# A state-space layer with a feed-forward behind it: opening loads reordered, the first state's sums in banks of their own, and block 1's first products moved

## Chip, cores and metric

One NeuronCore of a Trainium2 chip. The time is device time in microseconds of one execution of the whole program; the figure given for a kernel is the median of its runs. Engines are named as the profile names them: PE (TensorE, matrix products; PEld is its weight load), DVE (VectorE), ACT (ScalarE), POOL (GpSimd), and SP, from whose queue all loads and stores are issued. PSUM is the memory that PE writes to; the kernel uses eight banks of it, of 128 partitions x 512 floats, named by the tags f0 to f3, `o` (two), y0 and y1.

## What is computed

A chunked state-space recurrence (4 batches, 8 heads, 768 steps, head width 32, state width 16), whose result is turned to 3072 tokens x 256 and goes through a two-matrix feed-forward with the activation h * clip(h + 3, 0, 6) / 6. All in float32. The reference walks chunks of 32 steps:

```python
for c in range(nc):
    cum = np.cumsum(log_a[:, :, sl], axis=-1)
    L = np.exp(cum[:, :, :, None] - cum[:, :, None, :]) * causal
    M = np.einsum('bhin,bhjn->bhij', Cc, Bc) * L
    y_intra = np.einsum('bhij,bhjd->bhid', M, xc)
    y_inter = np.einsum('bhin,bhnd->bhid', Cc, state) * np.exp(cum)[:, :, :, None]
    y[:, :, sl] = y_intra + y_inter
    decay_from_j = np.exp(cum[:, :, -1:] - cum)
    Bx = np.einsum('bhjn,bhjd->bhjnd', Bc, xc) * decay_from_j[:, :, :, None, None]
    state = np.exp(cum[:, :, -1])[:, :, None, None] * state + np.sum(Bx, axis=2)
x = y.transpose(0, 2, 1, 3).reshape(B * S, H * D)
h = x @ w_in                                   # 3072 x 256 @ 256 x 2048
out = (h * np.clip(h + 3, 0, 6) / 6) @ w_out   # @ 2048 x 256
```

The two weight matrices arrive as float64.

## The kernel before

The 768 steps are cut into six chunks of 128 steps; a chunk of all four batches is a block of 512 tokens, and each block goes through the recurrence ("mixing") and then the feed-forward. The mixing of a block works in two halves of 64 steps. The order of all work is written by hand; each engine runs its instructions in the order in which the program names them, and waits where it needs another's result.

**Weights.** Each matrix is loaded as raw 64-bit words in four chunks of 1 MB (`raw`, three buffers) and decoded by hand to float32: `decode(i)` is a generator, and `weights(i, n)` runs its next n steps. Chunks 0 to 3 are w_in, 4 to 7 are w_out. The steps are a copy of the top 16 bits on ACT (L199, `ws`), an and/or on DVE (L202, `wm`), a product-sum on DVE (L206), two 16-bit steps on DVE (L216, L218), two activations on ACT (L222, L224), an or on DVE (L229, `we`) and the last product on DVE (L237), which writes w_in or w_out. For the first two chunks L202 and L206 come with the first step, for the others later. `load_w(i)` issues a chunk's load. The second chunk's load is held back: `load_w(1, behind=...)` lets POOL copy one column of a product L*cb into the buffer (L132), so that the load, which overwrites it, is not issued before that product is there. Loads 2 and 3 stand behind it on SP. From chunk 1 on, `decode` issues the load three chunks ahead itself (L224's step).

**Opening, chunk 0.** SP issues a, the first weights (L141), C, B, x. C comes by `pairs_first` in eight loads of 32 KB (L100), with runs of four steps together, B by `tokens_first` in one load of 256 KB (L93), in runs of 16 floats, x in one of 512 KB (L118). The decays L = exp(cum_i - cum_j) are made on PE: `diff_mask` (L337) starts eight banks, four for chunk 0 (tags f0 to f3) and four for chunk 1 (`o` twice, `y0`, `y1`), with the causal mask; `mask_again` (L344) writes two of them once more; `diff` adds the differences of the sums `cum`, which DVE has split into three bfloat16 parts (`split`); ACT takes the exponential (`diff_exp`, L366). `first_eto` makes exp(cum) of the second half (e_ps, L372 and L377). C is turned by DVE (`turn_squares`, L466, into csT) and parted by head into cT (`part_heads`, L473); B by four transposes on PE into t_ps (L423) and an ACT copy (L432, bT). POOL scales B by the decay to the half's end (`ends`, L397, bs).

Then `scores` (L523, cb = B C^T, in banks f0 to f3) with `into_state` at its end (L535: the sums of B x for both halves, which for chunk 0 lie in the second halves of the banks of y), and `multiply`: ACT takes the sums out (adds, mid), DVE makes L*cb in four instructions (L564), one for each pair of heads. `turn_cum` and `by_token` turn the sums cum (c_ps in f1, L317 and L320), `fade` scales half of csT (L479), `mix` makes y from L*cb and x (L589) and from the state (L501), `keep` copies it to yT (L603). Only then can the first feed-forward product start (`mlp_in`, L611), which also needs w_in's first chunk.

**Block 0's feed-forward.** For 16 columns f of w_in, `mlp_in` makes h on PE, ACT the ramp (L689), DVE the product (L694); the decode steps of chunks 2 to 6 are woven in by the table `weave`. Then `first_out(b, i)` makes the output (L705): four quarters i of w_out by four batches b. Between these calls, in the last loop of the program's first round, stands the mixing of chunk 1 and the preparation of what follows: `in_weight_sums` (L635: eight sums of w_in on DVE in two steps, four each), `weight_sums` (L732: four sums of w_out, one each step), `turn`, `wake`, `conceal` (POOL selects, L159), `scores`, `multiply`, `renew`, `decay_ends`, `results` (mix, keep and `sum_y`, L650).

**From block 1 on** the products are made by a scheme with seven instead of eight half products. `lead(k, s)` makes the first two of a step (bank `odd`) and copies them, on ACT into `even` (L668) and on DVE into `up` (L669); `early`, `middle` and `last` add the rest (all L653). `early(k, 0)` adds to `even`, so it needs ACT's copy. Block 0 calls `lead(1, 0)` after the last `first_out`.

Of the kernel before, what the change touches and what calls it, by code (L numbers as in the profile page):

```python
# [8 lines left out]
FP32 = mybir.dt.float32  # L9
# [11 lines left out]
def kernel(  # L21
# [63 lines left out]
    def load_bc(c):  # L85

        sl = slice(c * P, (c + 1) * P)

        def tokens_first(src, **where):
            t = loads.tile([P, NB * NH, N], FP32, **where)
            nc.sync.dma_start(out=t, in_=src[:, :, sl, :].rearrange("b h s n -> s (b h) n"))  # L93
            return t

        def pairs_first(src):
            t = loads.tile([P, 2, NB, 4, N], FP32, name="pairs", tag="bc")
            for b in range(NB):
                for h in range(2):
                    nc.sync.dma_start(  # L100
                        out=t[:, h, b].rearrange("s a n -> s (a n)"),
                        in_=src[b, h:NH:2, sl, :].rearrange("h (s a) n -> h s (a n)", a=4))
            return t

        if c == 0:
            bcs[c] = [pairs_first(C)]
        elif c < TURN:
            bcs[c] = [tokens_first(C, name="C", tag="bc")]
        Bs[c] = tokens_first(B, name="B")
        if c < TURN:  # L110
            bcs[c].append(Bs[c])
        else:
            bcs[c] = [pairs_first(C), pairs_first(B)]
# [14 lines left out]
    def load_w(i, behind=None):  # L128
# [13 lines left out]
        raws[i] = raw  # L142

    load_w(0)
    load_bc(0)
    load_x(0)
# [41 lines left out]
    def decode(i):  # L188
# [23 lines left out]
        if i < 2:  # L212
            next(parts_m)
            next(parts_m)
        yield
# [3 lines left out]
            out=s, in0=s, scalar1=0x8000, scalar2=None, op0=ALU.bitwise_and)  # L219
        next(parts_m, None)  # L220
        yield
# [119 lines left out]

    def mask_again(c, b):

        nc.tensor.matmul(  # L344
            out=ds[c, b], lhsT=ident_h, rhs=hide.unsqueeze(1).to_broadcast([P, NH, HT]),
            start=True, stop=True)

# [67 lines left out]
    def turn_ps(c, j):  # L415

        if c < 2:
            return ps.tile([P, NB, P], FP32, name="t_ps", tag=f"f{2 * j if c else 1}")
        return ps_o.tile([P, NB, P], FP32, name="t_ps", tag="o")
# [26 lines left out]
    def fade_c(c, t_ps):  # L446

        nc.vector.tensor_tensor(out=turned(c)[2], in0=t_ps, in1=etos[c], op=ALU.mult)

# [13 lines left out]

    def turn_squares(t, out):

        nc.vector.transpose(  # L466
            out=out.rearrange("r b (s a) -> r b a s", a=4),
            in_=t.rearrange("s t b a n -> s (b a) t n"))

    def part_heads(c):  # L470
        _, cT, csT = turned(c)
# [5 lines left out]
    def fade(c, sl=slice(0, P)):  # L477
        csT = turned(c)[2][:, :, sl]
        nc.vector.tensor_tensor(out=csT, in0=csT, in1=etos[c][:, :, sl], op=ALU.mult)  # L479

    def turn_all(c):
        bT, _, csT = turned(c)
        for t, out_ in zip(bcs[c], (csT, bT)):
            turn_squares(t, out_)
        part_heads(c)
        fade(c)

# [18 lines left out]
    def scores(c):  # L506
# [8 lines left out]
        ys[c] = {(0, u): both[u][:, 0] for u in range(2)}  # L515
        sps[c] = [both[a if c else 1 - a][:, 1] for a in range(2)]
        if c:
            from_state(c, 0)
        for b in range(NB):
            for a, rows in enumerate(HALF):  # L520
                for q in range(NQ):
# [4 lines left out]
                        tile_position=(32 * q, a * HT), skip_group_check=True)  # L526
        into_state(c, 0, 1)

# [24 lines left out]
    def multiply(c):  # L553

        take(c)
        mids[c] = mid = att.tile([P, NB, 2 * D], FP32, name="mid", bufs=1)
        if c == 0:
            for t in range(2):
                nc.scalar.activation(
                    mid[:, :, t * D:(t + 1) * D], sps[c][0][:, :, t * D:(t + 1) * D], AF.Copy,  # L560
                    scale=parity[:, t:t + 1])
        for q in range(NQ):
            hs = slice(2 * q, 2 * q + 2)
            nc.vector.tensor_tensor(  # L564
                out=Ls[c][:, :, hs], in0=Ls[c][:, :, hs], in1=cbs[c][q], op=ALU.mult)
            if c and q == 1:
                new_state(mid, sps[c][0], tmps[c])

    def renew(c):
# [127 lines left out]

    def first_out(b, i):

# [3 lines left out]
        o = outs[b // 2]  # L703
        for f in range(i * FP, (i + 1) * FP):
            nc.tensor.matmul(  # L705
                out=o[:, b % 2], lhsT=gTs[0][:, f, b * P:(b + 1) * P], rhs=w_out[:, f],
# [140 lines left out]

    for c in range(2):
        for b in range(NB):
            diff_mask(c, b)  # L850
    for sl in ends_at:
# [3 lines left out]
    in_three()  # L855
    for b in range(2):
        mask_again(0, b)
    diff(0, 0, 1)
    diff(0, 2, 3)
    turn_squares(bcs[0][0], turned(0)[2])  # L860
    part_heads(0)
    for b in range(NB):
        diff_exp(0, b)
    first_eto()
    weights(0, 1)
    add_up(ends_at[1])
    store_rows()
    diff(1, 2, 3)
    turn_b(0)
    for b in range(NB):  # L870
        ends(0, b)
    weights(0, 1)
    diff(1, 0, 1)
    diff_exp(1, 2)
    diff_exp(1, 3)
    weights(0, 2)
    scores(0)
    multiply(0)
    load_w(1, behind=Ls[0][:, 0, 2, :1])
    load_w(2)  # L880
    load_w(3)
    c_ps = ps.tile([P, NC, G], FP32, name="c_ps", tag="f1")
    turn_cum(c_ps)
    by_token(c_ps)
    busy(1, ps.tile([P, NB * P], FP32, name="d", tag="f0"))
    fade(0, HALF[1])
    weights(0, 1)
# [14 lines left out]
    for k in range(NC):  # L902
        gTs[k] = ffn.tile([P, NF, TB], FP32, name="gT")
        c, ahead = k + 1, k + 2
        if k == 0:
# [11 lines left out]
            for i in range(NP):  # L917
                for b in range(NB):
                    first_out(b, i)
                    if (i, b) == (0, 0):  # L920
# [4 lines left out]
                    elif (i, b) == (1, 0):  # L925
                        next(sums_in)
                    elif (i, b) == (2, 0):
                        turn(c, 1)
                        wake(c)
                        turn(c, 0)  # L930
                        for p in range(2):
                            conceal(ahead, p)
                    elif (i, b) == (2, 1):
                        next(sums_in)
                    elif (i, b) == (2, 2):
                        scores(c)
# [98 lines left out]
```

## Time and profile before

| What | us |
|---|---|
| median of 12 runs (362.51 to 364.1) | 363.25 |
| the profiled execution | 363.11 |
| its span on the core | 361.4 |
| PE busy | 349.6 |
| DVE busy | 225.3 |
| ACT busy | 177.4 |
| POOL busy | 140.0 |
| B of chunk 0 landed | 13.12 |
| first product of mlp_in | 23.31 |
| first product of first_out | 53.45 |
| first product of block 1 (lead) | 86.89 |

The span is the time from the first to the last instruction of the profiled execution; what lies around it is 1.7 us. PE counts as busy in 97% of the span, but a busy PE can be slower than it could be, and matmuls overlap. Times in the lower half of the table are microseconds from the span's start, in the timeline. A timeline line gives start, duration, engine, line, operation, out<-in, count, and in brackets the idle time of the engine before it with what ended that. The chain of work is followed back from the last instruction, at each step to what released it.

### The profile page before, as it was taken

The page shows a single profiled execution, that of the slowest core. Times are in us where ns is not written, and L with a number is a line of the kernel's source. Part 1 is how long each engine was busy: PE and PEld are TensorE (multiplying, and loading weights), DVE is VectorE, ACT ScalarE, POOL GpSimd, SP SyncE. Part 2 cuts the span into 40 slices and gives each one's busy share as a digit, 9 for nine tenths or more (in the row PEclk, how much of TensorE's full clock was granted, in tenths as well). Part 3 has the DMA queues.
Part 4 walks back from the last instruction along what each step waited for, and adds up shares of the span by engine and source line. Part 5 has one row for each costly group of instructions (what it writes and reads, how often), then busy time and mean ns, then how long its engine had stood idle before and what let it go on. Part 6 is the DMA issues. An engine that isn't in the chain of part 4 may idle for free.

```text
span 361.4 us, 9354 instructions
## 1 busy us (share of the span) xinstructions
PE 349.6 (97%) x3936; PEld 299.8 (83%) x3936; DVE 225.3 (62%) x427; ACT 177.4 (49%) x390; POOL 140.0 (39%) x139
## 2 busy tenths in 40 slices
PE   7698999999999999999999999999999999999996
PEld 3453448887888999888999888999888999888996
DVE  4778999996787634587436587535588421588111
ACT  4559878457666560576460476470476110476100
POOL 3300000182398712079722079820058700058700
PEclk9899999999999999999999999999999999999999
DMA  4979969902925043560034560000000000000000
GB/s 153 108 277 247 143 244 149 167 2 74 162 55 64 4 97 85 79 92 2 2 70 111 77 96 4 4 2 31 29 2 1 4 2 31 30 3 0 2 29 31
DMA packets 75482, 24.97 MB, mean 69 GB/s; under 512 B 66032, under 2 KB 71824, under 8 KB 74928
## 3 DMA queue, kind: packets, MB, share of 16 engines
q1 hardware_dynamic: 75440, 24.37, 34.9%
q8 instruction: 31, 0.51, 0.6%
q14 instruction: 11, 0.09, 0.1%
HBM read 21.07 MB, written 3.29 MB: 67 GB/s over the span
## 4 chain that ended last, share of the span: by engine, by line
PE 84%; DVE 7%; DMA 3%; ACT 3%; SPq 2%; issue 1%; POOL 0%; DVEq 0%; ACTq 0%
PE ob L764 18%; PE even L653 18%; PE oa L764 18%; PE odd L653 13%; PE o L705 8%; PE y L589 2%; PE h L611 2%; PE cb L523 2%; PE y L501 2%; DVE gT L694 2%; SPq L100 2%; DMA B<-in_B_dram 1%; DMA raw<-in_moe_w_in_dram 1%; PE y L535 1%; DVE wm L206 1%; ACT we L222 1%
## 5 line engine op out<-in xcount | busy, mean ns | idle before, releaser
L750 POOL TENSOR_TENSOR s<-gT 128x512 f32<-128x512 f32 x20 | 26.4, 1322 | 90.4 <-DVE gT L694 90.4
L653 PE MATMUL even<-ts,w_sum 128*128 128x256 f32 x160 | 48.2, 383 | 0.0
L668 ACT COPY even<-odd 128x512 f32<-128x512 f32 x40 | 23.0, 575 | 48.9 <-PE odd L653 46.7
L689 ACT ACTIVATE gT<-odd,half 128x512 f32<-128x512 f32 x40 | 27.5, 687 | 34.9 <-DVE odd L682 34.9
L653 PE MATMUL odd<-yT,w_in 128*128 128x256 f32 x160 | 41.1, 379 | 0.0
L764 PE MATMUL oa<-w_out,gT 128*128 128x128 f32 x320 | 38.9, 277 | 0.0
L764 PEld LDWEIGHTS oa<-w_out,gT 128*128 128x128 f32 x320 | 38.1, 192 | 0.9
L764 PE MATMUL ob<-w_out,s 128*128 128x128 f32 x320 | 37.4, 275 | 0.0
L764 PEld LDWEIGHTS ob<-w_out,s 128*128 128x128 f32 x320 | 36.5, 192 | 0.0
L653 PEld LDWEIGHTS even<-ts,w_sum 128*128 128x128 f32 x160 | 29.9, 190 | 5.3 <-ACT up L675 1.5
L694 DVE SCALAR_TENSOR_TENSOR gT<-gT,odd 128x512 f32<-128x512 f32 x40 | 27.5, 688 | 9.9 <-ACT gT L689 9.9
L653 PEld LDWEIGHTS odd<-yT,w_in 128*128 128x128 f32 x160 | 30.1, 190 | 3.9
L386 ACT ACTIVATE L<-L,cum_n 128x64 f32<-128x64 f32 x128 | 31.1, 336 | 0.5 <-POOL L L159 0.5
L764 PE MATMUL ob<-t,gT 128*128 128x128 f32 x240 | 30.3, 279 | 0.0
L611 PE MATMUL h<-yT,w_in 128*128 128x512 f32 x64 | 28.4, 599 | 1.8 <-DVE gT L694 1.4
L689 ACT ACTIVATE gT<-even,half 128x512 f32<-128x512 f32 x40 | 27.8, 695 | 4.4 <-PE even L653 4.4
L694 DVE SCALAR_TENSOR_TENSOR gT<-gT,even 128x512 f32<-128x512 f32 x40 | 27.2, 679 | 4.4 <-ACT gT L689 4.4
L669 DVE COPY up<-odd 128x256 f32<-128x256 f32 x40 | 17.0, 425 | 20.4 <-ACT even L668 19.6
L764 PEld LDWEIGHTS ob<-t,gT 128*128 128x128 f32 x240 | 27.9, 192 | 1.2 <-issue 0.5
L705 PE MATMUL o<-w_out,gT 128*128 128x256 f32 x128 | 28.6, 381 | 0.0
L705 PEld LDWEIGHTS o<-w_out,gT 128*128 128x128 f32 x128 | 24.0, 190 | 4.0 <-ACT gT L689 0.8
L159 POOL TENSOR_SCALAR_AFFINE_SELECT L<-L 64x1024 f32<-64x1024 f32 (+1 forms) x16 | 19.8, 1242 | 17.4 <-DMA L<-cum_d 17.1
(130 smaller groups left out, 611.2 us busy)
## 6 DMA issues: line engine op xcount, KB each, us to landing
raw<-in_moe_w_in_dram SPq DMA_DIRECT2D x4, 1024.0 KB
raw<-in_moe_w_out_dram SPq DMA_DIRECT2D x4, 1024.0 KB
L<-cum_d SPq DMA_DIRECT2D x8, 512.0 KB
xt<-in_x_dram SPq DMA_DIRECT2D x6, 512.0 KB
out_dram<-res SPq DMA_DIRECT2D x20, 128.0 KB
B<-in_B_dram SPq DMA_DIRECT2D x6, 256.0 KB
eto<-cum_e SPq DMA_DIRECT2D x20, 64.0 KB
pairs<-in_C_dram SPq DMA_DIRECT2D x32, 32.0 KB
```

The source lines that it names most:

```text
L100: nc.sync.dma_start(out=t[:, h, b].rearrange("s a n -> s (a n)"), in_=src[b, h:NH:2, sl, :].rearrange("h (s a) n -> h s (a n)", a=4))
L159: nc.gpsimd.affine_select(out=t[rows], in_=t[rows], pattern=pattern, compare_op=ALU.is_ge, fill=-1e5, base=base, channel_multiplier=-1)
L386: nc.scalar.activation(Ls[c][:, b, h], Ls[c][:, b, h], AF.Exp, bias=cum_n[:, c, g:g + 1])
L611: nc.tensor.matmul(out=h.rearrange("p r i -> p (r i)"), lhsT=w_in[:, j, f * P:(f + 1) * P], rhs=yTs[k][:, j].rearrange("p b i -> p (b i)") ...
L653: nc.tensor.matmul(out=bank[:, r], lhsT=lhsT, rhs=rhs, start=start, stop=True, skip_group_check=True)
L668: nc.scalar.copy(out=even, in_=odd[:, 1:2].to_broadcast([P, 2, 2 * P]))
L669: nc.vector.tensor_copy(out=up[:, 1], in_=odd[:, 0])
L689: nc.scalar.activation(gTs[k][:, f], h.rearrange("p r i -> p (r i)"), AF.Relu, bias=half, scale=1.0 / 6.0)
L694: nc.vector.scalar_tensor_tensor(out=g, in0=g, scalar=1.0, in1=h.rearrange("p r i -> p (r i)"), op0=ALU.min, op1=ALU.mult)
L705: nc.tensor.matmul(out=o[:, b % 2], lhsT=gTs[0][:, f, b * P:(b + 1) * P], rhs=w_out[:, f], start=(f == 0 and b % 2 == 0), stop=True, skip_ ...
L750: nc.gpsimd.tensor_tensor(out=o, in0=p_, in1=q_, op=op)
L764: nc.tensor.matmul(out=bank[:, slot], lhsT=lhs[:, j], rhs=rhs[:, j], start=(clear and j == 0), stop=True, skip_group_check=True)
```

## The change

SP's opening order becomes a, C, B, the first weights, x. C of chunk 0 is now loaded by `tokens_first`, in one load of the shape of B's, and turned on PE through PSUM as chunk 1's is; `turn_squares`, `part_heads` and `fade` are gone as functions of their own. `fade_c` scales only the second half for chunk 0. At the start only six banks get their mask; ten masks of 192 columns are laid over one of them; the two banks `o` of chunk 1 get theirs after the scores, and their differences then. For chunk 0 `into_state` is taken out of `scores` and comes in `first_state`, into banks f2 and f3. `times_scores` is one of the four products of `multiply`; for chunk 0 they are called two by two, with decode steps between. For the first weight chunk only L202's step comes at the beginning. The stores of the sums (`store_rows`) are named after the second and third weight loads. In block 0's last loop both steps of `in_weight_sums` come at (1, 0), `scores` one call later, and `lead(1, 0)` inside the last `first_out`, ahead of its last two columns.

```diff
     def load_bc(c):
-        if c == 0:
-            bcs[c] = [pairs_first(C)]
-        elif c < TURN:
+        if c < TURN:
             bcs[c] = [tokens_first(C, name="C", tag="bc")]
...
+    load_bc(0)
     load_w(0)
-    load_bc(0)
     load_x(0)
...
         if i < 2:
             next(parts_m)
+        if i == 1:
             next(parts_m)
         yield
...
-        next(parts_m, None)
+        if i:
+            next(parts_m, None)
         yield
...
-    def mask_again(c, b):
+    def mask_again(c, b, h):
         nc.tensor.matmul(
-            out=ds[c, b], lhsT=ident_h, rhs=hide.unsqueeze(1).to_broadcast([P, NH, HT]),
-            start=True, stop=True)
+            out=ds[c, b][:, h:h + 3], lhsT=ident_h,
+            rhs=hide.unsqueeze(1).to_broadcast([P, 3, HT]), start=False, stop=True,
+            skip_group_check=True)
...
     def fade_c(c, t_ps):
-        nc.vector.tensor_tensor(out=turned(c)[2], in0=t_ps, in1=etos[c], op=ALU.mult)
+        sl = slice(0, P) if c else HALF[1]
+        nc.vector.tensor_tensor(
+            out=turned(c)[2][:, :, sl], in0=t_ps[:, :, sl], in1=etos[c][:, :, sl], op=ALU.mult)
...
-        into_state(c, 0, 1)
+        if c:
+            into_state(c, 0, 1)
...
+    def times_scores(c, q):
+        hs = slice(2 * q, 2 * q + 2)
+        nc.vector.tensor_tensor(
+            out=Ls[c][:, :, hs], in0=Ls[c][:, :, hs], in1=cbs[c][q], op=ALU.mult)
+
+    def first_state():
+        sps[0] = [ps.tile([P, NB, 2 * D], FP32, name="sp", tag=f"f{2 + a}") for a in range(2)]
+        into_state(0, 0, 1)
+        mids[0] = mid = att.tile([P, NB, 2 * D], FP32, name="mid", bufs=1)
+        for t in range(2):
+            nc.scalar.activation(
+                mid[:, :, t * D:(t + 1) * D], sps[0][0][:, :, t * D:(t + 1) * D], AF.Copy,
+                scale=parity[:, t:t + 1])
+        take(0)
...
         for f in range(i * FP, (i + 1) * FP):
+            if b == NB - 1 and f == NF - 2:
+                lead(c, 0)
             nc.tensor.matmul(
...
-    for c in range(2):
-        for b in range(NB):
-            diff_mask(c, b)
+    for b in range(NB):
+        diff_mask(0, b)
+    for b in range(2, NB):
+        diff_mask(1, b)
...
-    for b in range(2):
-        mask_again(0, b)
+    for _ in range(10):
+        mask_again(1, 2, 0)
     diff(0, 0, 1)
+    t_ps = turn_ps(0, 0)
+    turn_c(0, t_ps)
     diff(0, 2, 3)
-    turn_squares(bcs[0][0], turned(0)[2])
-    part_heads(0)
     for b in range(NB):
         diff_exp(0, b)
     first_eto()
-    weights(0, 1)
+    turn_b(0)
+    diff(1, 2, 3)
+    fade_c(0, t_ps)
     add_up(ends_at[1])
-    store_rows()
-    diff(1, 2, 3)
-    turn_b(0)
     for b in range(NB):
         ends(0, b)
-    weights(0, 1)
-    diff(1, 0, 1)
     diff_exp(1, 2)
     diff_exp(1, 3)
-    weights(0, 2)
+    weights(0, 1)
     scores(0)
-    multiply(0)
+    times_scores(0, 0)
+    times_scores(0, 1)
     load_w(1, behind=Ls[0][:, 0, 2, :1])
     load_w(2)
-    load_w(3)
+    store_rows()
+    weights(0, 1)
+    times_scores(0, 2)
+    times_scores(0, 3)
+    for b in range(2):
+        diff_mask(1, b)
+    diff(1, 0, 1)
     c_ps = ps.tile([P, NC, G], FP32, name="c_ps", tag="f1")
     turn_cum(c_ps)
+    busy(1, ps.tile([P, NB * P], FP32, name="d", tag="f0"))
+    weights(0, 2)
+    load_w(3)
+    first_state()
     by_token(c_ps)
-    busy(1, ps.tile([P, NB * P], FP32, name="d", tag="f0"))
-    fade(0, HALF[1])
     weights(0, 1)
     mix(0)
...
                     elif (i, b) == (1, 0):
                         next(sums_in)
+                        next(sums_in)
...
-                    elif (i, b) == (2, 1):
-                        next(sums_in)
-                    elif (i, b) == (2, 2):
+                    elif (i, b) == (2, 3):
                         scores(c)
                         multiply(c)
                         renew(c)
                         decay_ends(ahead, 0)
+                        decay_ends(ahead, 1)
                         next(sums)
-                    elif (i, b) == (2, 3):
-                        next(sums)
-                        decay_ends(ahead, 1)
                     elif (i, b) == (3, 0):
                         next(sums)
                         decay_ends(ahead, 2)
                     elif (i, b) == (3, 1):
                         results(c)
+                        next(sums)
                         decay_ends(ahead, 3)
+                    elif (i, b) == (3, 3):
                         from_start(ahead)
-                    elif (i, b) == (3, 3):
-                        lead(c, 0)
```

More of the change, by code (lines that the diff above doesn't have):

```diff
@@ L415, in turn_ps @@
     def turn_ps(c, j):
-        if c < 2:
-            return ps.tile([P, NB, P], FP32, name="t_ps", tag=f"f{2 * j if c else 1}")
+        if c == 1:
+            return ps.tile([P, NB, P], FP32, name="t_ps", tag=f"f{2 * j}")
         return ps_o.tile([P, NB, P], FP32, name="t_ps", tag="o")
@@ L462, in wake, with turn_all @@
             ends(c, b)
[L464 to L471, printed above, removed]
+    def turn_all(c):
+        bT, cT, csT = turned(c)
+        for t, out_ in zip(bcs[c], (csT, bT)):
+            nc.vector.transpose(
+                out=out_.rearrange("r b (s a) -> r b a s", a=4),
+                in_=t.rearrange("s t b a n -> s (b a) t n"))
         for t in range(2):
@@ L475, in part_heads @@
                 op0=ALU.mult)
[L477 to L486, printed above, removed]
+        nc.vector.tensor_tensor(out=csT, in0=csT, in1=etos[c], op=ALU.mult)
     def busy(n, bank):
@@ L515, in scores @@
         ys[c] = {(0, u): both[u][:, 0] for u in range(2)}
-        sps[c] = [both[a if c else 1 - a][:, 1] for a in range(2)]
         if c:
+            sps[c] = [both[a][:, 1] for a in range(2)]
             from_state(c, 0)
@@ L556, in multiply @@
         mids[c] = mid = att.tile([P, NB, 2 * D], FP32, name="mid", bufs=1)
[L557 to L561, printed above, removed]
         for q in range(NQ):
[L563 to L566, printed above, removed]
+            times_scores(c, q)
+            if q == 1:
                 new_state(mid, sps[c][0], tmps[c])
+    def times_scores(c, q):
[11 more added lines that the diff above has]
+        take(0)
     def renew(c):
@@ L696, in times_ramp, with first_out @@
             op1=ALU.mult)
-    def first_out(b, i):
+    def first_out(b, i, c):
         if i == 0 and b % 2 == 0:
@@ L918 @@
                 for b in range(NB):
-                    first_out(b, i)
+                    first_out(b, i, c)
                     if (i, b) == (0, 0):
```

## Prediction

> **What bounds the kernel now.** I read the page's chain of work first, then the chain in order of time, then the timeline of the opening and of the step from block 0 to block 1. The chain's shares by engine:
>
> ```profile
> PE 84%; DVE 7%; DMA 3%; ACT 3%; SPq 2%; issue 1%; POOL 0%; DVEq 0%; ACTq 0%
> ```
>
> TensorE (PE) carries most of the span and its work is not changed, so time can come only from stretches where the chain is on something else. In order of time (start, us, what) these lie in the first 46 us:
>
> ```profile
> 7.17 0.53 SPq L100
> 7.70 0.04 issue
> 7.74 5.37 DMA B<-in_B_dram
> ...
> 16.14 1.50 PE cb L523 x63
> 17.63 0.01 issue
> 17.64 1.30 DVE L L564 x2
> 18.94 0.05 issue
> 18.99 0.20 POOL raw L132
> 19.19 0.02 issue
> 19.21 5.25 DMA raw<-in_moe_w_in_dram
> 24.46 0.02 issue
> 24.48 0.70 DVE wm L202
> ...
> 46.35 7.13 PE h L611 x16
> 53.49 15.74 PE o L705 x72
> ```
>
> The reader is to see one string: eight C loads issued on SP, then B, which lands at 13.12; the scores cb; two products L*cb; the POOL copy that lets the second weight chunk's load go; its landing at 24.46; and its decode on VectorE (DVE). From there DVE is busy nearly without a pause (4.8 of 5 us in 30-35, 9.76 of 10 in 50-60), and PE follows it. So I call S the start of the first L*cb (17.64) and T the start of decode 1 (24.48). What T moves, all behind it moves.
>
> The DMA queue (SP, timeline; start, duration) shows what a load of 4096 packets costs:
>
> ```profile
> 7.74 0.48 SPq L93 DMA_DIRECT2D B<-in_B_dram  x1
> 8.27 3.82 SPq L118 DMA_DIRECT2D xt<-in_x_dram  x1
> ```
>
> B takes 5.38 us from issue to landing, and the load behind it gets off the queue only at 12.09, 4.35 after B's issue began.
>
> **The opening, part by part.** *Loads.* Removed from SP: eight C issues (1.74 to 7.70). Added: one C load shaped like B. It takes the first weights' place at 1.27 and lands at 1.27 + 5.38 = 6.65. B's issue then ends at 1.27 + 4.35 = 5.6, and B lands 4.90 later (13.12 less its issue's end at 8.22): b = 10.5. The first weights stand behind B; B's packets fade out 4.3 after its issue's end (half-microsecond windows: 17 GB/s in 11.5-12, 9 in 12-12.5), so at 9.9; then 1 MB at the 393 to 418 GB/s that the same load showed at 4-5 us is 2.6: w = 12.6. x follows: its 3.2 us of packets (12.9 to 16.0 now) and about 0.7 to land give 16.5. No row shows C and B first on an empty queue, so bounds: below, both flow without the tail (B's bulk took 2.2 of its 3.5 us, so 1.3 less each): B's issue ends at 4.3, b = 7.9 and w = 4.3 + 3.0 + 2.6 = 9.9; above, nothing overlaps, w = 1.27 + 5.38 + 5.38 + 5.25 = 17.3. I take the middle, because the queue's own 4.35 shows that the next load starts before the last one landed.
>
> The trace has 64-byte pieces at 129 to 161 GB/s in B's middle. [...]
>
> *Work up to S.* C is turned by PE: four transposes (0.60 by the warm row at 69) enter ahead of the second pair of decay differences and push e_ps and its exponential from 10.07 to 10.67; DVE loses the stream transpose (1.08) and pays 1.49 for two cT products out of PSUM (0.74 each at 102.6) instead of 0.88, all of it before 10.7, hidden while it waits for the exponential. Then on DVE the half fade 0.42, the scan 1.42 (ends 12.5) and the first decode step 0.69, which waits for w. In DVE order these now stand ahead of L*cb. On PE from b: transposes of B 0.60, differences of two batches 1.16 (7.69 to 8.85), scores 0.98 (warm, at 120.2) = 2.74. So S = max(10.5 + 2.74, max(12.5, 12.6) + 0.69) = 13.3. The floor is 13.2, whatever the loads do.
>
> PE now idles from 10.20 to 13.25, and its granted clock then reads 0.50 from 13.5 to 16.5: scores 1.52 instead of 0.98. The new gap is 9.8 to 10.5, filled ahead by ten short masks that end before the split (6.5). By the row 0.7 us of idling is harmless; if B lands after 12.8, 3 us idle again, S is 0.5 later. [...]
>
> *S to T.* The load's string as now: 1.30 + 0.05 + 0.20 + 0.02 + 5.25 = 6.84 with the gaps. DVE's own string grows, since decode 0 is cut up: L*cb 1.30, the two 16-bit steps 1.08, L*cb 1.18, L206's product 1.31, c_ps 0.28, L229 0.69, L237 1.23 = 7.07. It has replaced a wait (2.0 before 24.48). T = 13.3 + 7.1 = 20.4, against 24.48: **4.1 us earlier**. POOL's four bs (3.6 from b) end at 14.1, before its copy is due at 14.6.
>
> *Covers.* The state sums leave the scores (0.86) and come after L*cb has freed their banks (S + 3.6 = 16.9, x there by 16.5); mid 0.63, mixing and keeping (20.40 to 23.30 now, 2.9) end at 20.4, with w_in chunk 0 ready at 20.4. If x were 1 us later, PE would start chunk 0 that much later, and half of it would be covered: from 20.4 chunk 0's products (16 at 0.43) last to 27.3, while chunk 1 is there at T + 7.4 = 27.8, as 24.48 goes to 31.84 now. Masks and differences of chunk 1 (two batches) move behind the scores, into PE time that waits for DVE. The cum stores now wait on SP behind two weight loads; their first reader is at 27.
>
> **The step to block 1.** The timeline:
>
> ```profile
> 74.29 1.52 DVE L635 TENSOR_TENSOR w_sum<-w_in,w_sum 128x512 f32<-128x512 f32 x1
> 75.73 1.63 DVE L635 TENSOR_TENSOR w_in<-w_in 128x512 f32<-128x512 f32 x1
> ...
> 86.89 1.03 PE L653 MATMUL odd<-yT,w_in 128*128 128x256 f32 x4
> 88.01 0.57 ACT L668 COPY even<-odd 128x512 f32<-128x512 f32 x1 [0.33 <-PE odd L653]
> 88.63 0.70 PE L653 MATMUL even<-yT,w_in 128*128 128x256 f32 x2 [0.71 <-ACT even L668]
> ```
>
> lead() now leaves two products of the last output (four PE rows at 3.62/16, 0.90) behind itself, which cover the 0.71 in which PE waits for ACT's copy: between 0 and -0.7; I take -0.7, since t3 is ready at 86.07. Against it: all eight sums of w_in now stand ahead of csT on DVE. csT (0.69) starts not at 72.01 but after four more sums: 71.3 + 2.75 at the free 0.69 each, or + 4.74 as they ran beside POOL's selects. PE wants it after one more group of eight rows (73.49 + 1.81 = 75.30). The wait is 0 to 1.4; only the last sum meets the selects, so csT ends near 75.7: +0.4. Sum -0.3. Moving from_start behind the copy costs ACT's queue 0.6 where nothing waits: tmp on POOL, then idle to 93.4.
>
> **Sum.** -4.1 - 0.3 = -4.4 on the profiled execution (363.11; span 361.4) gives 358.7; the median is 0.14 higher: **358.9**.
>
> **The rivals.**
> - *Loads half serial.* C and B tails add up (a later C load faded for 2 us at 28 to 49 GB/s), w = 14.5 to 15.5, S near 15.7, T 22.8: -1.7, with the step -2.0: 361.2. For it: such tails; against: B's single load.
> - *Slower: the weights behind everything.* DVE's first decode step stands before L*cb, so w gates the second chunk. From w = 24.48 - 7.07 - 0.69 = 16.7 on, the opening loses. At the upper bound 17.3, T = 25.1: +0.6, with the csT wait at 1.1 net +0.4: 364.2. Against: the queue's overlap of 1 us per load.
> - *No change: the gain is given back.* If w_out's raw loads did not move up, decode would wait for them. Chunk 1's packets end at 46.5 and its first reader is at 50.50, a slack of 4.0 that would just be used up; but their issues hang on decode itself (26.58 right after L206 at 26.50). 363.2.
>
> **How the numbers follow.** Forecast 0.68, half serial 0.17, no change 0.04, slower 0.11. What this kernel's measurement can tell is 0.2%, 0.7 us: faster 0.85, same 0.04, slower 0.11. The likeliest case alone spans 358.4 (S at the floor, -4.2, and no csT wait, -0.7) to 359.9 (-4.1, csT 1.4). The range goes 0.8 below that, for a DVE string with the later, shorter durations of the same rows (0.42 for 0.56 and 0.52, 1.22 for 1.31), which takes 0.3, and 0.5 of what a measurement spreads; above, it takes in the half-serial case up to T = 23.5: 357.6 to 362.2.
>
> **What would show it.** B's transposes on PE at 10 to 11; first L*cb near 13.3; the second weights' load issued near 14.8 instead of 19.21; decode 1 at 20.4; PE's h run after it at 27.7 instead of 31.84; o at 49.4 instead of 53.49; no wait on ACT's copy where block 1 begins; a wait for csT at the scores of block 1 under 0.5. It would be wrong if the first decode step starts after 15, or the o run starts earlier but the end does not.

## The result and the profile after

The changed kernel takes 365.37 us (median of 11 runs, 364.64 to 366.24) against 363.36 us (47 runs of the kernel before on the same chip): a ratio of 1.0054, interval 1.0042 to 1.0066. It is slower by 2.0 us, where 4.4 less was forecast. Its profiled execution took 364.25 us with a span of 362.5, so it shows 1.1 us of loss (364.25 less 363.11); the rest lies between that execution and the median.

The page's chain of waits has fewer waits in it than before, and more time:

```profile
span 362.5 us, 9363 instructions
...
PEclk9858999999999999999999999999999999999999
...
PE 93%; DVE 3%; issue 1%; ACT 1%; DMA 1%; DVEq 0%; ACTq 0%
```

PE's share of the chain went from 84% to 93%: what was removed was indeed removed from the chain. But PE's clock row now has a 5 in its third slice (18 to 27 us; a digit is tenths of full speed), and the chain in order of time shows what stands there (start, us, what):

```profile
11.07 1.14 PE cb L514 x63
12.21 0.54 PE d L336 x2
12.74 0.43 PE d L349 x2
13.17 0.53 PE d L358 x25
13.70 2.24 issue
15.94 0.42 PE d L358 x7
16.36 0.56 PE c_ps L316 x4
16.92 2.00 PE d L482 x2
18.93 1.08 PE sp L527 x62
...
20.04 0.73 PE y L590 x49
20.77 1.20 issue
21.97 0.46 PE y L590 x14
...
25.64 29.59 PE h L612 x64
55.23 15.54 PE o L709 x72
```

From 11 us to the o products nothing but PE is on the chain, and PE stops twice: 2.24 us within a row of 32 equal small products (25, then 7), and 1.20 us within one of 64 mixing products. The releaser is "issue", which means that the profile shows nothing that PE waited for. The scores start at 11.00 instead of 16.07, yet the feed-forward starts 2.3 us later than before (25.57 in the timeline, 23.31 before).

The loads and DVE did what was forecast. From the timeline (start, us, engine, line, operation; in brackets the idle time before it and what ended it):

```profile
11.98 0.69 DVE L199 TENSOR_SCALAR wm<-raw 128x1024 uint32<-128x1024 uint32 x1
12.59 1.28 DVE L556 TENSOR_TENSOR L<-L,cb 128x512 f32<-128x512 f32 x2
19.75 0.69 DVE L199 TENSOR_SCALAR wm<-raw 128x1024 uint32<-128x1024 uint32 x1 [0.64 <-DMA raw<-in_moe_w_in_dram]
25.57 5.62 PE L612 MATMUL h<-yT,w_in 128*128 128x512 f32 x8
25.96 1.11 ACT L196 COPY ws<-raw 128x1024 uint16<-128x1024 uint16 x1
27.10 0.43 DVE L214 TENSOR_SCALAR we<-ws 128x1024 uint16<-128x1024 uint16 x1 [5.33 <-ACT ws L196]
```

S, the first L*cb, is at 12.59 and T, decode 1, at 19.75. But decode 1 then stands still for 5.33 us, since its ACT copy (L196) is queued behind ACT's copies of yT, which wait for the late mixing. It costs nothing more here: from 25.57 on PE is not idle for more than 0.1 us at a time until 288.13.

How the granted clock goes, in half-microsecond windows (window, length, then busy time of PE, weight loads, DVE, ACT and POOL, then the clock, the DMA share and GB/s):

```profile
13.50:14.00 0.50, 0.20 (x13) 0.09 (x5) 0.50 (x2) 0.00 (x0) 0.07 (x1) 1.00 1.46 134
15.50:16.00 0.50, 0.06 (x2) 0.06 (x4) 0.50 (x2) 0.50 (x1) 0.00 (x0) 0.82 0.59 110
16.00:16.50 0.50, 0.50 (x9) 0.44 (x10) 0.50 (x1) 0.50 (x1) 0.00 (x0) 0.50 1.10 270
29.00:29.50 0.50, 0.50 (x2) 0.34 (x1) 0.00 (x0) 0.50 (x1) 0.00 (x0) 0.52 0.44 127
29.50:30.00 0.50, 0.50 (x2) 0.19 (x1) 0.08 (x1) 0.50 (x2) 0.00 (x0) 1.00 0.92 360
```

PE ran at half clock from the end of the first stop until 29.5, over 13 us. Its work in the mixing took longer for that: the two filling products L482 2.08 us instead of 1.13, and 64 mixing products 1.18 instead of 0.86, both beside the run with the loads held (below), whose clock was at full there.

The step to block 1 went as forecast. In the timeline the last four products of block 0's output stand behind lead(), and PE no longer waits for ACT's copy:

```profile
87.55 1.03 PE L654 MATMUL odd<-yT,w_in 128*128 128x256 f32 x4
88.41 1.03 PE L709 MATMUL o<-w_out,gT 128*128 128x256 f32 x4
88.73 0.60 ACT L669 COPY even<-odd 128x512 f32<-128x512 f32 x1
89.38 0.70 PE L654 MATMUL even<-yT,w_in 128*128 128x256 f32 x2
```

**Where the time went, stage by stage** (kernel after less kernel before, starts in the timeline): first h +2.26 (25.57 and 23.31); first o +1.61 (55.06 and 53.45); turning B for chunk 1 +1.54 (70.61 and 69.07); first even product of block 1 +0.75 (89.38 and 88.63); end of the span +1.1. All of the loss is there at the first h. Afterwards 0.7 comes back up to turning B, since PE no longer waits for DVE in the feed-forward (1.40 and 0.36 in the kernel before), less what the half clock costs there until 29.5, and another 0.8 at the step; of the 0.35 lost behind it, 0.15 is a wait at 288.13 that comes up below.

### The profile page after: what moved, and what is told of

It is laid out like the page before. It is cut to its first block, busy times and chain, and to the rows that moved or that the text cites. A ratio compares the mean times of both kernels' runs of the same rounds, so it can differ in the third digit from the quotient of the medians.

```text
span 362.5 us, 9363 instructions
## 1 busy us (share of the span) xinstructions
PE 352.8 (97%) x3948; PEld 302.9 (84%) x3948; DVE 223.1 (62%) x426; ACT 177.9 (49%) x390; POOL 137.6 (38%) x139
## 4 chain that ended last, share of the span: by engine, by line
PE 93%; DVE 3%; issue 1%; ACT 1%; DMA 1%; DVEq 0%; ACTq 0%
PE ob L768 18%; PE even L654 18%; PE oa L768 17%; PE odd L654 13%; PE h L612 8%; PE o L709 8%; PE y L590 3%; PE y L492 2%; PE cb L514 2%; PE y L527 1%; PE d L358 1%; DMA pre<-in_a_dram 1%; PE d L482 1%; PE t_ps L423 1%; PE d L349 1%
## 5 line engine op out<-in xcount | busy, mean ns | idle before, releaser
L612 PE MATMUL h<-yT,w_in 128*128 128x512 f32 x64 | 29.7, 626 | 0.0
L404 POOL TENSOR_TENSOR tmp<-state,eto 128x256 f32<-128x256 f32 x5 | 3.3, 660 | 65.4 <-DMA eto<-cum_e 58.2
```

The source lines that it names most:

```text
L612: nc.tensor.matmul(out=h.rearrange("p r i -> p (r i)"), lhsT=w_in[:, j, f * P:(f + 1) * P], rhs=yTs[k][:, j].rearrange("p b i -> p (b i)") ...
```

## What PE waited for

The largest queue on the page besides that of the loads is "q8 instruction", 31 packets, 0.51 MB, alike in both kernels. 0.51 MB by 31 is 16 KB a packet. In the stretches 12 to 13 and 19 to 20 us of the kernel after there is one such packet each. The DMA view of the second (queue, kind: packets, MB, share of the engines):

```profile
q1 hardware_dynamic: 101, 0.39, 100.4%
q8 instruction: 1, 0.02, 6.4%
```

PE's instructions can be counted in the trace in the order of their starts: weight loads, products, and the few semaphore waits of PE's own queue. The first stop lies before the 449th, the second before the 705th: 256 apart. And in the opening a packet of the instruction queue begins after PE has passed the 193rd, the 449th, the 705th. The theory (A in the expectations) is therefore: PE gets its program in blocks of 256 instructions; as it enters one (at 193 + 256k) the next is sent for; if it comes late, PE stops where the next one should begin. Worked out from the trace, in us:

```
kernel   block from   sent for   packet      delay   needed   stop
before   449           9.69      10.26-11.66  0.57    17.54    none
before   705          17.54      18.27-19.20  0.73    21.10    none
before   961          21.10      25.26        4.16    37.10    none
after    449           9.74      12.95-14.47  3.21    13.70    to 15.94
after    705          15.94      19.66-20.67  3.72    20.77    to 21.97
```

No record tells when a block is sent for; the column gives the start of the 193rd, 449th or 705th instruction, as the theory has it. "Delay" is from there to the packet's start, and PE goes on 1.3 to 1.5 after its end. In the kernel before, the first fetch, by this column, stood beside packets of 64 bytes alone (1267 of them in its 0.57 us), and PE had 7.85 us (9.69 to 17.54) for the 256 instructions of a block, 3.1 of which it waited for B. In the kernel after it used up the block in 3.96 us, and the fetch took 6.2: beside the rest of the first megabyte of weights (until 11.2) and then x at first, beside the second and third megabyte the next time.

The rivals tested against it: B, a wait of some other kind at that place in the program (a buffer, a semaphore that the profile doesn't show); C, that the step to block 1 costs the time.

## The experiments

All start from the kernel after unless it is said, and the kernel before ran beside them; ratios are to it.

**Forty more instructions.** If A holds, the stops must move to other products when only the number of instructions ahead of them changes. Ten masks of 192 columns become thirty of 64: the same columns, 40 PE instructions more.

```diff
-            out=ds[c, b][:, h:h + 3], lhsT=ident_h,
+            out=ds[c, b][:, h:h + 1], lhsT=ident_h,
...
-    for _ in range(10):
+    for _ in range(30):
         mask_again(1, 2, 0)
```

> The changed kernel with its ten masks of 192 columns cut into thirty of 64: the same columns, 40 more PE instructions (20 weight loads, 20 products) ahead of everything that matters. Theory A (PE runs out of instructions: its stream comes in blocks of 256 by DMA, and in the changed kernel the fetch of a block stands behind the weights and x): both PE stalls keep their instruction number and so come 40 instructions earlier in the work: the first after about 5 of the 32 small products of the two late batches instead of after 25, the second some 20 products earlier in the mixing; time within 1 us of the changed kernel's 365.4. Theory B (an unseen wait for another engine's result at that place): the stalls stay after product 25 and in the middle of the mixing.

Its PE timeline:

```profile
13.41 0.28 PE L358 MATMUL d<-split,pick 128*64 128x64 bf16 x5
15.70 0.80 PE L358 MATMUL d<-split,pick 128*64 128x64 bf16 x27 [2.01 <-issue]
...
19.88 0.72 PE L590 MATMUL y<-L,xt 64*32 64x64 f32 x29
23.16 0.79 PE L590 MATMUL y<-L,xt 64*32 64x64 f32 x34 [2.56 <-issue]
```

The first stop now comes after 5 of the 32 small products instead of 25 (20 products and 20 weight loads earlier), the second after 30 of 64 instead of 50. Both are again at the 449th and the 705th. Theory B falls: no buffer and no semaphore moved. The time, 367.1 in one run, is higher than expected: the second packet was delayed by 4.98 instead of 3.72, and that stop grew to 2.56, and a third one of 0.77 stands at 86.9.

**Hold the other loads back.** The loads of weight chunks 1 to 3 go to where chunk 0 is decoded, so that no load stands in the way of the second fetch.

```diff
-    load_w(1, behind=Ls[0][:, 0, 2, :1])
-    load_w(2)
...
-    load_w(3)
...
+    load_w(1, behind=w_in[:, 0, :1])
+    load_w(2)
+    load_w(3)
```

> The changed kernel with the loads of weight chunks 1 to 3 held until the first chunk is decoded (about 19 instead of 14.3). Theory A: the block fetched from 16 to 20 no longer stands behind them, so the stall in the mixing (1.2 us) goes or falls under 0.4, while the first (2.2) stays; PE begins the feed-forward 1 us or more earlier than 25.6; decode 1 starts at 24 to 25; time 362.8 to 364.8. Theory B: the stall in the mixing stays at 1.2, and the later weights make the kernel slower than 365.4.

365.10 (10 runs), ratio 1.0041 [1.0022, 1.0061], above the 362.8 to 364.8 expected. Its timeline:

```profile
15.96 0.31 PE L358 MATMUL d<-split,pick 128*64 128x64 bf16 x7 [2.06 <-issue]
...
19.91 0.34 PE L590 MATMUL y<-L,xt 64*32 64x64 f32 x14 [0.92 <-issue]
...
22.19 7.13 PE L612 MATMUL h<-yT,w_in 128*128 128x512 f32 x16
...
24.99 0.69 DVE L199 TENSOR_SCALAR wm<-raw 128x1024 uint32<-128x1024 uint32 x1 [5.78 <-DMA raw<-in_moe_w_in_dram]
```

The delay of the second packet falls from 3.72 to 1.32 (15.96 to 17.28), and h starts at 22.19 instead of 25.57. The second stop doesn't fall away as expected, since PE comes to the 705th at 18.99 now. The clock stayed at 1.00 until 32 after a first stop of nearly the same length. What it wins there it loses by the late load: decode 1 is at 24.99, and PE idles 3.03 for it at 32.

**The step alone, and the opening alone.** The kernel before with the second part of the change (lead() ahead of the last output products, the sums of w_in ahead of csT), and the kernel after with the old step.

```diff
+            if b == NB - 1 and f == NF - 2:
+                lead(c, 0)
...
-                        from_start(ahead)
-                        lead(c, 0)
+                        from_start(ahead)
```

> The kernel before with the second part of the change alone (block 1's first products ahead of the last two columns, scores one call later, both sets of weight sums early). Theory A: the whole loss is in the opening, and this part gains 0.7: 362.7. Theory C (the step to block 1 costs): 363.4 or more.

> The changed kernel with the step to block 1 as in the kernel before. Theory A: 0.7 slower than the changed kernel, 366.1. Theory C: at or under 365.0.

The step alone: 363.00 (12 runs), ratio 0.9987 [0.9973, 1.0000], a gain of 0.5 us at the edge of what can be told. The opening alone: 366.19 (4 runs), ratio 1.0080 [1.0055, 1.0104]. Theory C falls: the whole loss is in the opening, and the step gives back 0.8 of it (366.19 less 365.37).

**x ahead of the first weights.** A load of small packets (x's are of 128 bytes in the kernel after, the weights' of 4096) in the megabyte's place when the first fetch, by the theory, is sent for; the decode of chunk 0 moves behind L*cb.

```diff
+    load_x(0)
     load_w(0)
-    load_x(0)
...
-    weights(0, 1)
...
-    weights(0, 1)
...
+    weights(0, 2)
```

> The changed kernel with x loaded ahead of the first weights, and that chunk's first decode steps named after the products L*cb, so that they don't wait for it. Theory A (block fetches wait behind big packets, not behind small ones): the block asked for at about 9.7 now stands behind x's small packets, its data start within 1.3 us instead of 3.2, and the stall in the small products (2.2 us) goes or falls under 0.6; the next block, asked for at about 13.6, stands behind the first weights, so that a stall of 0 to 1.5 us in the mixing stays; feed-forward begins at 21 to 23.5 instead of 25.6; time 360.5 to 363.5. If the big packets were not the cause, the first stall stays at 2 us and the later weights make it 366 or more.

363.68 (10 runs), ratio 1.0003 [0.9989, 1.0017], just above the 360.5 to 363.5 expected. Its PE timeline:

```profile
14.32 0.31 PE L358 MATMUL d<-split,pick 128*64 128x64 bf16 x7 [0.56 <-issue]
...
20.90 0.46 PE L590 MATMUL y<-L,xt 64*32 64x64 f32 x14 [3.54 <-issue]
```

The first delay is halved (1.66 instead of 3.21) and the first stop is 0.56; but the second fetch is now sent for at 14.32, just as the second and third chunk's loads have been issued, waits 4.10, and PE stops for 3.54, where 0 to 1.5 was expected. Half clock follows from 19.8 to 30. The order of the loads moved the stop from one block to the next here (2.24 and 1.20 us in the kernel after, 0.56 and 3.54 now).

**Change the count so that the second block begins elsewhere.** First with 28 masks of 64 columns (36 instructions more) on the kernel with x first; then with 96 early instructions more in the order of the kernel after, two batches of differences moved into the feed-forward, and three filling products instead of one.

```diff
-    for _ in range(10):
+    for _ in range(28):
         mask_again(1, 2, 0)
```

```diff
-            out=d, lhsT=ident_h, rhs=hide.unsqueeze(1).to_broadcast([P, NH, HT]),
-            start=True, stop=True)
...
+                out=d[:, h:h + step], lhsT=ident_h,
+                rhs=hide.unsqueeze(1).to_broadcast([P, step, HT]), start=(h == 0), stop=True,
...
+                if f == 3:
+                    for b in range(2):
+                        diff_mask(1, b, late=True)
+                    diff(1, 0, 1)
```

> The same with 28 masks of 64 columns instead of ten of 192, 36 more PE instructions ahead, so that the mixing ends before the block after next is needed (block ends at instruction 449, 705, 961). Theory A: as the run with x first, with at most one stall, in the mixing, under 1.5 us; time within 0.7 of it, 360.5 to 363.5.

> The changed kernel (its load order kept) with its PE instructions moved so that each block is asked for before big packets stand ahead of it: the six first masks cut in eight pieces each and 16 masks of 128 columns (96 instructions more at the start), the late differences of two batches of chunk 1 (72 instructions) moved into the feed-forward after column 3, and three filling products instead of one. Theory A: both stalls under 0.3 us, no half clock after 16, feed-forward from 20 to 22, and the gain forecast for the opening comes: 358.5 to 361.0. If the stalls are not bound to instruction blocks, or if the half clock or ACT's order alone make the loss: 363 or more.

Both missed: 367.30 (4 runs), ratio 1.0099 [1.0082, 1.0116], and 370.75 (4 runs), ratio 1.0194 [1.0170, 1.0217]. In the first, PE stopped three times, at the 449th (0.74), the 705th (17.51 to 20.73) and the 961st (23.58 to 26.80; here the profile names ACT as the releaser, but the block's packet ran from 24.53 to 25.53, and PE went on 1.3 after it as at the other stops). In the second:

```profile
11.61 0.95 PE L517 MATMUL cb<-cT,bT 32*64 32x128 f32 x45
14.69 1.11 PE L517 MATMUL cb<-cT,bT 32*64 32x128 f32 x19 [2.13 <-issue]
```

The block was sent for 1.7 us earlier (8.05), but the first weights' packets had begun at 7.8, and it was delayed by 3.84. The stop had only moved on to the scores, where L*cb waits for it. With more instructions the 961st also comes earlier: PE stopped for 2.45 there (the profile names ACT as the releaser, as above). Not all of the 370.75 is stops: the filling products took 4.66 us at mostly half clock (2.08 in the kernel after). Neither count helped, and in the second the stop went with what the load queue did at that moment.

**The kernel before with its loads issued early.** If A holds, the kernel before owes its freedom from stops to a quiet load queue at 17.5. Two loads are moved to behind x, nothing else.

```diff
+    load_w(1)
+    load_w(2)
...
-    load_w(1, behind=Ls[0][:, 0, 2, :1])
-    load_w(2)
```

> The kernel before with the loads of weight chunks 1 and 2 issued behind x at the start, instead of being held back until the second product L*cb. Theory A: the block that PE asks for at about 17.5 now waits 2.5 us or more behind them (0.7 before), and a stall of 0.5 to 2.5 us appears in the mixing, where the kernel before has none; decode 1 begins 2 us earlier, so that the time says little: 361.5 to 365. If big packets don't hold the fetch: no stall, and 361.5 to 362.5.

366.03 (4 runs), ratio 1.0067 [1.0043, 1.0091], above the 361.5 to 365 expected; the stop came where it was expected. Its PE timeline:

```profile
20.95 0.95 PE L591 MATMUL y<-L,xt 64*32 64x64 f32 x62
23.94 0.36 PE L591 MATMUL y<-L,xt 64*32 64x64 f32 x2 [2.04 <-issue]
```

The second packet's delay goes from 0.73 to 3.36 (18.08 to 21.45), and PE stops for 2 us in the mixing of a kernel that never stopped there; its row before is

```profile
20.40 0.97 PE L589 MATMUL y<-L,xt 64*32 64x64 f32 x64
```

None of the changed kernel's order is in it. This is the plainest test: early loads alone made the stop, of 2.04 us.

**Loads timed around the fetch.** The second chunk's load is released just after the second fetch, by the theory, has been sent for. With x first, it is held to the last L*cb or to the first weights' landing; with the order of the kernel after, to the cumulative sums at 17 (cum_n).

```diff
-    load_w(1, behind=Ls[0][:, 0, 2, :1])
+    load_w(1, behind=Ls[0][:, 0, 6, :1])
```

```diff
-    load_w(1, behind=Ls[0][:, 0, 2, :1])
+    load_w(1, behind=raws[0].bitcast(FP32)[:, :1])
```

```diff
-    load_w(1, behind=Ls[0][:, 0, 2, :1])
-    load_w(2)
...
-    load_w(3)
+    load_w(1, behind=cum_n[:, 2, :1])
+    load_w(2)
+    load_w(3)
```

> The run with x first (e5), with weight loads 1 and 2 held until the last of the four products L*cb instead of the second (about 15 instead of 13.9). PE asks for its block at 14.3. Theory A: if that is ahead of the load's issue, the block's data start by 16.5 instead of 18.4 and the stall in the mixing falls from 3.5 to under 1 us; feed-forward begins at 21 to 23 instead of 24.5; time 360.5 to 362.5. If the load still comes first, the stall stays above 2 us and the time at 363 to 364.5.

> The same, with weight loads 1 and 2 held until the first weights have landed (about 16.5). Theory A: the block is fetched ahead of them for certain, stall under 1 us, feed-forward from 22 to 23, decode 1 from 22 to 23: 360.3 to 362, faster than both kernels. If the opening's shorter loads don't help even without stalls: 363 or more.

> The changed kernel with its load order, and the weight loads 1 to 3 held until cum_n is there (about 17.3 instead of 14.3). Theory A: the first stall (2.2) stays, the second is at 1.2 or less, as in the run that held them to 19.5; decode 1 begins at 22.5 instead of 25: 360.5 to 363.5, with a spread of 2 us or more where the half clock comes or not.

Beside these three the kernel before had a median of 364.44 (29 runs), so the ratios tell more than the times. Last product: 363.14 (10 runs), 0.9971 [0.9952, 0.9990]. First weights: 362.95 (12 runs), 0.9963 [0.9946, 0.9981]. Cumulative sums: 362.61 (12 runs), 0.9962 [0.9944, 0.9979]. All three are faster than the kernel before by 0.3 to 0.4%, and so than the kernel after; the two with x first stay above their expected 360.5 to 362.5 and 360.3 to 362. The second packet's delay is 1.21, 1.20 and 1.25 in them. With x first, two stops of 0.5 to 0.8 remain, and then PE waits 2.5 to 2.7 for mid on ACT, which stands behind chunk 0's late decode there. The third one's timeline:

```profile
16.23 0.31 PE L358 MATMUL d<-split,pick 128*64 128x64 bf16 x7 [2.37 <-issue]
...
19.54 1.12 PE L590 MATMUL y<-L,xt 64*32 64x64 f32 x63
...
22.60 7.13 PE L612 MATMUL h<-yT,w_in 128*128 128x512 f32 x16
23.35 0.69 DVE L199 TENSOR_SCALAR wm<-raw 128x1024 uint32<-128x1024 uint32 x1 [4.11 <-DMA raw<-in_moe_w_in_dram]
```

The first stop is still there, the second is gone, h starts at 22.60 (23.31 before) and decode 1 at 23.35 (24.48 before). Its span is 360.7 against 361.4. It has the lowest ratio found, though the intervals of the three overlap: 1.4 us below the kernel before (0.0038 of 364.44), where 4.4 was forecast for the change.

## Why the prediction was wrong

- **C, B and the first weights land earlier: right.** B was being turned at 9.38 (forecast b = 10.5), the first weights' decode starts at 11.98 (w = 12.6). The splitting of C into 64-byte pieces cost nothing that shows: the 8192 such packets of C and B together ran from 2.35 to 7.77.
- **S and T: right.** 12.59 for 13.3, and 19.75 for 20.4; T is 4.7 earlier, not 4.1. S even came below the 13.2 that the prediction called a floor whatever the loads do: csT started at 10.50 and the scan took 1.20 instead of 1.42, so that it ended at 12.0, not 12.5. The second load was issued at 14.28 for 14.8.
- **The gap of PE before the scores: right as far as it went.** It is gone. But the sentence that 0.7 us of idling is harmless (in the kernel before the clock stayed at 1.00 after the 0.71 ahead of 88.63) looked for the gap where the kernel before had it; a new one of 2.24 us, three times as long, opened at 13.70, behind the scores. Half clock followed it, from 15.82 to 29.48, and cost 3.1 us up to h by the estimate below, where 0.5 was forecast for a gap of 3 us.
- **"Covers": wrong, and the step that failed.** It put the state sums at 16.9 and the feed-forward at 20.4, and took for granted that PE runs its products as soon as data and buffers are there. The state sums began at 18.86 and the feed-forward at 25.57. Of these 5.2 us the two stops are 3.44 (2.24 + 1.20). The half clock is the rest and more: from the first stop's end to h PE took 9.63 less 1.20 = 8.4 us in the kernel after, and 6.23 less 0.92 = 5.3 with the loads held and the clock at full, a difference of 3.1. Both together are 6.5: without them, by this estimate, PE would have been ready at 19.1, with w_in, which was there at 19.1 (17.88 + 1.23), ahead of the 20.4 of the forecast. T didn't move "all behind it", because behind T now stood PE.
- **The step to block 1: right in sign, its wait mis-sized.** -0.3 was forecast from a gain of 0.7 and a wait for csT of 0.4. The wait was 0, and the step gave 0.79 between turning B and the even product in the traces, 0.5 and 0.8 in the two kernels that had it alone or lacked it.
- **The sum** was -4.1 - 0.3. What came of it in the profiled executions is +1.54 up to block 1, -0.79 and +0.35 behind it (1.1), and 2.0 in the medians. The 0.9 between these is not explained by a profile: the profiled execution is below every one of the 11 timed runs. The half clock alone doesn't explain it: the six runs whose mean granted clock was 0.979 to 0.981, like that of the profiled execution (0.981), took 365.24 to 366.24, those at 0.986 364.87 to 365.47, and the two at 0.991 364.64 and 364.67. So the time goes with the length of the half clock, by about 1 us; how long the stops were in those runs isn't recorded.
- **The rivals.** None of the three was it. The slower one asked for weights later than 16.7, and they came before 12. That PE itself could become the bound in the opening was not among them; the chain of the kernel before gave no sign, as its PE has no stop of 0.1 us or more with the releaser "issue". The queue of the instructions stood on the page, with the same 31 packets.

Not settled: why the fetch, on a queue of its own (q8; the loads are on q1), is later when loads run on another. The runs show that the two go together (in the first three fetches of each run, a delay of 0.4 to 2.2 where almost nothing but packets of up to 512 bytes moved meanwhile, 1.2 to 5.0 where the weights' packets of 4 KB did) but not at which point. Nor did any run keep the first stop from occurring with the order C, B, weights, x; moving the count alone did not do it, and splitting or holding the first megabyte was not tried.

## What to carry to other kernels

Count PE's instructions in stretches of small products: 256 of them lasted 3.96 us in the kernel after (9.74 to 13.70), and the packet that by the theory brings the next was over only at 14.47, with the loads running. So a load that is moved earlier, or a wait of PE's that is removed, is to be looked at against the instruction packets too; the sign in these runs was a PE that was idle for 0.53 to 3.54 us in the middle of equal products, with the releaser "issue". Here it paid to release the next big load only after the fetch had been sent for (18.05 instead of 14.28 us in the last run), though the load then lands later.

## What was unexpected about the hardware

- The stops stand 256 PE instructions apart, or a multiple of it. Those in the opening were at the 449th, 705th and 961st in all kernels that stopped, whatever product that was. Late ones fit too: PE's only wait over 0.1 us in the last 270 us of the kernel after (0.15 at 288.13) and of the last version (0.66 at 286.35, a part of its gain given back) is before the 6593rd, which is 193 + 25 x 256, and the 0.77 at 86.9 in the kernel with forty more instructions is before the 1985th, 193 + 7 x 256. In the run with 96 early instructions more, 1.19 at 181 and 1.20 at 248 us come before the 4033rd and the 5825th, 193 + 15 and 22 x 256. The places are counted in the traces; the moment of asking is the author's estimate from the opening alone, and during long products a packet was also seen well ahead of it (27.67 in the kernel after, where PE passes the 961st at 34.90). What a packet of 16 KB holds, no trace shows; that each brings a block of 256 is the author's estimate from these places and from the packets that end 1.3 to 1.5 us ahead of PE's going on.
- Similar stops cost the clock differently: 2.24 us in the kernel after was followed by 13.7 us at half clock, 2.37 (loads behind the cumulative sums) by 3.4, and 2.06 (loads held) by none. The windows show what goes with it. In the traces the changes of clock lie 3.41 us or a multiple of it apart: half clock in the opening lasts 3.41 in the kernel before (13.33 to 16.74), 6.83 with 96 early instructions more (14.36 to 21.18), 10.24 with x first (19.76 to 30.00) and 13.66 in the kernel after (15.82 to 29.48). So the trace can be cut into stretches of that length. Two stretches each of the kernel after, of the run with the loads held and of the last run (PE's busy time is the second number, the clock the third from the end):

```profile
12.41:15.82 3.41, 1.29 (x29) 0.64 (x27) 3.38 (x8) 2.27 (x3) 0.32 (x1) 1.00 1.00 100
15.82:19.24 3.42, 3.30 (x45) 1.67 (x46) 3.25 (x5) 0.75 (x1) 0.00 (x0) 0.50 0.96 345
11.82:15.23 3.41, 2.09 (x69) 1.14 (x58) 3.38 (x7) 2.27 (x3) 0.00 (x0) 1.00 1.27 136
15.23:18.65 3.42, 2.69 (x116) 1.85 (x119) 3.39 (x6) 1.62 (x3) 0.00 (x0) 1.00 0.12 27
13.63:17.04 3.41, 1.04 (x27) 0.85 (x20) 3.38 (x6) 2.30 (x2) 0.00 (x0) 1.00 0.50 67
17.04:20.45 3.41, 3.41 (x130) 1.91 (x129) 2.16 (x4) 0.58 (x3) 0.58 (x1) 0.50 0.41 86
```

  With the loads held, the stop is split between two stretches (PE busy 61% and 79%), and the clock stays; in the other two it lies in one (38% and 31%), and the next is at half clock. Other stretches at full clock go the same way, but for the two between 50% and 55%. Half clock followed one with PE busy 11% in the kernel before (9.92 to 13.33), 29% with x first (16.35 to 19.76), 47% with 96 instructions more (10.95 to 14.36), 40% in the kernel before with its loads early (20.63 to 24.04) and 55% with 36 more (19.21 to 22.62). Full clock followed stretches of 82% (16.74 to 20.16) and 59% (30.40 to 33.81) in the kernel before, and one of 50% (15.80 to 19.21) with 36 more. In these runs the full clock came back after a stretch in which PE was busy 99% or more, which suggests that the second stop, too, made the half clock longer (65% in its stretch). This is read from traces; no run was made to test it, and a stretch of 100% was not always enough (22.65 to 26.06 in the kernel after).
- A fetch that by the theory was sent for early could come later: at 8.05 its delay was 3.84, at 9.74 it was 3.21, and at 9.69 on a quieter queue 0.57.
